# Earlier lanes, a two-pass ring for the last four groups, and scalings on VectorE in a fused attention and feed-forward kernel

## The chip, the cores and the metric

The kernel runs on one core of a Trainium2 chip. The metric is the device time of one execution in microseconds (us); the time before is the median of three runs. A profile is one further execution, recorded by the hardware profiler; times in it count from the start of its span. The engines are named as in the profile: PE is TensorE's matmuls, PEld its weight loads, DVE is VectorE, ACT is ScalarE, POOL is GpSimd, and SP is the engine that issues most DMAs.

## The reference

```python
x: (4, 12480, 128)  inducing: (32, 128)  w_in: (128, 2048)  w_out: (2048, 128)  alpha: (2048)
def mab(q, kv):
    a = softmax(q @ kv.T / sqrt(128))
    return a @ kv
h   = mab(inducing, x)         # per batch: 32 rows pool 12480 tokens
y   = mab(x, h)                # each token attends to the 32 rows
z   = y @ w_in
g   = max(z, 0) + alpha * min(z, 0)
out = g @ w_out                # (49920, 128), f32
```

## The kernel before

The kernel never forms `y`. It computes `hW = h @ w_in` once per batch (32 rows, repeated four times over the 128 partitions) and, for each token, the unnormalised weights `rep` of the 32 rows (also held four times). A product of a quarter of each, 32 rows deep, gives a chunk of 128 of the 2048 features for 512 tokens. The activation is split as `alpha*z + (1-alpha)*max(z,0)`, so the linear part needs one further product with `hA = h @ (w_in * alpha @ w_out)`, and only the relu part needs the 2048 features. The division by the softmax sum is left to the end, where it multiplies the output.

**Units.** Each batch has 25 groups: 24 of 512 tokens (numbers 0 to 23; four of them, one super tile, share their loads) and a remainder of 192 tokens (number 24). A group has 16 chunks. `fill` (L596) makes a chunk: one matmul on a quarter of the array (32 rows) into one of eight banks, and then a relu that brings it to bf16 in SBUF, on ScalarE (L614) or VectorE (L617). The planner keeps a clock for the three engines and gives the relu to the engine that it thinks is done first, from durations written by hand (`ca`, `cd` at L611). `piece` (L621) multiplies a chunk with the scaled output weights and adds to the group's own bank. A whole chunk can be summed in one full matmul of 128 rows (`whole`, L627), or in four quarter matmuls of 32 rows, one at a time.

**Lanes.** Quarter matmuls on the four row groups of the array run at the same time. Each row group is a lane. A laned group enters lane 0, has its 16 chunks' first quarters added there, then goes to lane 1 for the second quarters, and so on; up to four groups are in the lanes at once, one in each. Two lanes must not add to one bank at once, so before a group goes on, TensorE drains (L969, `hand_over`) and the first piece of the next lane waits for that drain's semaphore. Fills use slots of any lane. A chunk stays in SBUF until lane 3 has used it; at most `KEPT` are held. The loop from L976 chooses the next matmul by the planner's clock; `PLAN` has one letter per laned group, which sets four knobs of that choice (how hungry the eviction engines must be for a fill to go first, how many chunks may be left in lane 3 when a new group starts, what a fill costs an occupied lane, and whether a hand-over is made at once).

**Direct groups.** The first two groups, the four remainders, and groups 22 and 23 of batch 3 are direct, with whole sums. At the start there are eight *sessions* (L921): four fills at once, some tasks, then the four whole sums of the session before. A ninth set of four fills follows, and then the lanes begin. At the end, after the lanes have run empty, groups 22, 23 and 24 of batch 3 are summed whole (L1101); their fills are made before, in free lane slots.

**Tasks.** All other work (scores of the next super tile, its sums, loads and transposes for the next batch) stands in a table by time step, `at(t, ...)`. Steps up to 8 are the sessions; step T0 + m comes when the m-th laned group starts. If a step has matmuls, lanes pause there, because these matmuls use the whole array. At the start, `w_amat` (16 matmuls for `w_in * alpha @ w_out`), `h_linear` and the first two transposes of batch 1 stand in sessions.

**Finishing** (`finish`, L653): VectorE transposes the bank to SBUF (L664), GpSimd multiplies with the reciprocal sums (L667), and four DMAs write the result (L685). In the last batch DMAs of the last groups are issued by SP and ScalarE, and two of group 23 at the very end by GpSimd (L688). GpSimd also issues the loads of x.

Of the kernel before, what the change touches and what calls it, by code (L numbers as in the profile page):

```python
# [17 lines left out]
P = 128  # L18
NB = 4
GRP = P * NB  # L20
# [4 lines left out]
TAIL = 2  # L25
AHEAD = 8
LAND = 8000
KEPT = 62
RDS = 4
SLOT = 217  # L30
XTS = 9
DONE = 420
SWITCH = 110
# [4 lines left out]
PLAN = (  # L38
    "aaKKfGcyLqmADMamiiznjafamQcyaqcafqanqaxacmOaav"
    "AmnCamKeacfymraaJmRnAynqyauaNmmgadjmafycQazyAm"  # L40
)
# [3 lines left out]
def kernel(  # L45
# [550 lines left out]
    def fill(ch, f):  # L596
        b, g, u = ch
        st = states[b]
        pp, nb, cp = shape_of(g)
        t = pp * nb  # L600
        w = t * cp
        ps = bank()
        for i in range(cp):
            mm(
                ps[:, i * t : (i + 1) * t],
                st.hW[32 * f : 32 * f + 32, u * cp + i, :],
                st.rep[g][32 * f : 32 * f + 32, :t],
            )
        gt = gt_pool.tile([P, GRP], bf16, name="gt", tag="gt")
        after = 206 + w * 0.42  # L610
        ca, cd = 52 + w * 0.83, 74 + w * 1.04  # L611
        ready = clk.pe + after
        if max(clk.act, ready) + ca <= max(clk.dve, ready) + cd:
            pin(nc.scalar.activation(out=gt[:, :w], in_=ps[:, :w], func=RELU))  # L614
            drained(ps, "A", ca, after=after)
        else:
            pin(nc.vector.tensor_relu(gt[:, :w], ps[:, :w]))  # L617
            drained(ps, "D", cd, after=after)
        seen[ch] = gt, clk.free[number[id(ps)]]
# [28 lines left out]

    def flush():
        while held:  # L650
            finish(*held.pop(0))

    def finish(b, g):  # L653
        st = states[b]
# [9 lines left out]
        pin(nc.vector.transpose(out=ot[:, :t], in_=acc[:, :t]))  # L664
        drained(accs[b, g], "D", 74 + t * 1.04)
        ob = ob_pool.tile([P, GRP], f32, name="ob", tag="ob")
        pin(nc.gpsimd.tensor_tensor(  # L667
            out=ob[:, :t].rearrange("p (k m c) -> p k m c", k=nb, c=32),
# [153 lines left out]
    def tokens(st):  # L822
# [15 lines left out]
        tail = [y for y in direct[2:] if y[0] == B - 1]  # L838
# [21 lines left out]
        at(4, lambda: b_turn(st, 0))  # L860
        at(5, w_amat)
        at(6, lambda: h_linear(st))
        for b in range(B):
            base = T0 + (first[b, 0] if b else -2)
            for s in range(1, NS + 1):
                t = base + 4 * s - AHEAD - (b == 0 and s > 4) if b or s > 2 else 4 * s - 2
                nt = t + (5 if b == 0 and s == 2 else 3 if b == 0 and s == 4 else 4 if s < NS or b + 1 < B else 2)
                at(t, lambda b=b, s=s: b_scores(states[b], s))
                at(t + 1, lambda b=b, s=s: b_rep(states[b], s))
                at(nt, lambda b=b, s=s: b_den(states[b], s))  # L870
                at(nt + 1, lambda b=b, s=s: b_turn(states[b], s))
            if b + 1 < B:
                n = b + 1
                E = base + 4 * NS
                if b:
                    lag = (-8, -4, -4, 0, 4, 8, 8) if b > 1 else (-4, 0, 0, 4, 4, 8, 8)
                    score = [base + k for k in lag]
                    load = [t + k - 7 for t, k in zip(score, (0, 0, 2, 0, 1, 0, 2))]
                    cross = [t + k - 5 for t, k in zip(score, (0, 0, 1, 0, 1, 0, 2))]
                else:  # L880
                    score = [T0 + k for k in (2, 4, 4, 6, 9, 11, 13)]
                    load = [0, 0, 5, SESSIONS, T0 + 2, T0 + 4, T0 + 6]
                    cross = [None, None, 6, T0 + 1, T0 + 4, T0 + 7, T0 + 8]
# [4 lines left out]
                sums = [T0 + k for k in (4, 6, 6, 9, 11, 13, 14)] if n == 1 else [k + 4 for k in score]  # L888
                fs, fa = (t_scores, t_accum) if n == 1 else (a_scores, a_accum)
# [31 lines left out]
        for t in range(SESSIONS):  # L921
# [8 lines left out]
            prior = now  # L930
        for f in range(2):
            linear(0, f, f)
# [5 lines left out]
        finish(*held.pop(0))  # L938
        run_tasks(SESSIONS)
        flush()  # L940

# [12 lines left out]
        assert len(plans) == len(laned)  # L954
        fresh = {f: bank() for f in (2, 3)}

# [9 lines left out]
        def hand_over():  # L966
            nonlocal fenced
            if owed:
                pin(nc.tensor.drain(fusable=True)).then_inc(fence, 1)  # L969
                fenced += 1  # L970
            for y, f in owed:
                fences[y, f + 1] = fenced
                moving.append((y, f + 1, clk.pe + DONE))
            owed.clear()

        while queue or moving or owed or any(tile):  # L976
            best = []
            taken = {q for _, q, _ in moving} | {f + 1 for _, f in owed}
            for f in range(4):
                if tile[f]:  # L980
                    y, todo = tile[f]
                    if todo[0] is None:
                        best.append((free_at[f], 0, f, "linear"))
                    elif (*y, todo[0]) in seen:
                        t = max(free_at[f], seen[*y, todo[0]][1] - 100)
                        best.append((t, 1, f, "piece"))
                else:
# [4 lines left out]
                    if f == 0 and queue and lanes < LANES and (  # L992
                        lanes < LANES - 1 or room == KC or tile[3] and len(tile[3][1]) <= room
                    ):
                        ch = (*queue[0], 0)
                        if ch in seen:
                            t = max(free_at[f], seen[ch][1] - 100 - SLOT)
                            best.append((t, 2, f, "start"))
            if fillable():
                since = max(min(clk.free[i] for i in idle) - 40, landed.get(need[0][:2], 0))  # L1000
                hungry = min(clk.act, clk.dve) < clk.pe + hungry_at
                for f in range(4):
                    t = max(free_at[f], since)
                    if hungry:
                        best.append((t, 0.5 + 0.1 * bool(tile[f]), f, "fill", cost if tile[f] else 0))
                    elif not tile[f]:
                        best.append((t, 4 + (f in taken), f, "fill"))
            soon = min(max(x[0], clk.pe) for x in best) < clk.pe + 2 * SLOT
            for f in sorted(fresh):
# [7 lines left out]
            calm += [x for x in best if x[3] in ("warm", "spare")]  # L1017
            if owed and not best:
                hand_over()
                continue  # L1020
            if owed and not calm and at_once:
# [16 lines left out]
            if what == "start":  # L1038
# [34 lines left out]
            if what == "fill":  # L1073
                fill(need.pop(0), f)
            else:
                y, todo = tile[f]
                u = todo.pop(0)
                if u is None:
                    linear(*y, f)
                else:  # L1080
                    ch = (*y, u)
# [4 lines left out]
                    if f == 3:  # L1086
                        seen.pop(ch)
                    if not todo:
                        tile[f] = None
                        if f < 3:  # L1090
                            owed.append((y, f))
                        flush()
            free_at[f] = clk.pe + SLOT
# [51 lines left out]
```

## Time and profile before

| | us |
|---|---|
| median of 3 runs (559.07 to 559.81) | 559.15 |
| the profiled execution | 558.86 |
| its span | 557.1 |
| first fill | 25.38 |
| lanes begin | 41.7 |
| lanes end | 541.7 |
| last matmul ends | 550.6 |
| relus to SBUF: ScalarE 923, mean | 0.620 |
| relus to SBUF: VectorE 645, mean | 0.676 |
| transpose of a finished group, VectorE, mean of 96 | 0.710 |
| product with reciprocal sums, GpSimd, mean of 96 | 1.133 |

Means are durations of one instruction; those of an engine overlap, so that they follow each other a little faster. A matmul's duration includes its way through the array; the pace is seen in the starts. All of the helper `mm`'s matmuls have the line L138, so they are told apart by what they read: `rep,hW` is a fill, `gt,W` a piece or a whole sum, `W` alone an unneeded matmul in an empty lane.

### The profile page before, as it was taken

The numbers are of one execution on the slowest core, as the hardware profiler recorded it, in microseconds if no ns is written. First come the engines' busy times: TensorE is split into PE (matmuls) and PEld (weight loads), VectorE is DVE, ScalarE is ACT, GpSimd is POOL, SyncE is SP. The second block draws the span as 40 slices with busy tenths as digits, with TensorE's granted clock in tenths as the row PEclk, the third lists the DMA queues.
The fourth block names the chain that finished last, engine by engine and source line by source line (L and its number), as shares of the span: only waits on it lengthen the run. The fifth ranks groups of instructions, "written<-read, shape, count | busy, mean of one in ns | idle before, by whom it ended". The sixth has DMA issues, their size and how long they took to land.

```text
span 557.1 us, 21434 instructions
## 1 busy us (share of the span) xinstructions
PE 538.6 (97%) x8890; PEld 293.1 (53%) x8894; DVE 497.3 (89%) x858; ACT 503.8 (90%) x1008; POOL 411.4 (74%) x602
## 2 busy tenths in 40 slices
PE   4999999999999999999999999999999999999995
PEld 4645555555455555544555556554465554454642
DVE  3689999989999999999998999999998999999981
ACT  2479999999989999999999999999999999999980
POOL 6556466967898978878698878665668859767683
PEclk9999999999999999999999999999999999999999
DMA  9976999645999998687577996333334334333224
GB/s 196 230 136 142 134 192 176 132 94 89 151 199 165 176 144 164 148 120 150 102 131 131 169 170 140 64 93 88 75 81 112 73 81 118 65 94 65 47 62 75
DMA packets 110209, 69.25 MB, mean 124 GB/s; under 512 B 78800, under 2 KB 100672, under 8 KB 110112
## 3 DMA queue, kind: packets, MB, share of 16 engines
q0 software_dynamic: 23344, 38.66, 37.6%
q1 hardware_dynamic: 84624, 28.46, 26.3%
q8 instruction: 69, 1.13, 0.9%
q10 hardware_dynamic: 2144, 0.77, 0.5%
q14 instruction: 28, 0.23, 0.2%
HBM read 41.00 MB, written 28.95 MB: 126 GB/s over the span
## 4 chain that ended last, share of the span: by engine, by line
PE 31%; issue 27%; PEld 25%; POOL 8%; DMA 4%; ACT 3%; DVE 1%; PEldq 1%; POOLq 0%; DVEq 0%
PE bank L138 31%; PEld L138 25%; POOL out_dram L685 5%; DMA xn<-in_x_dram 3%; POOL ob L667 3%; ACT gt L614 2%; PEldq L969 1%; PE bank L226 1%; DMA out_dram<-ob 1%; DVE gt L617 1%; DVE hW L313 0%; POOL xn L180 0%; DVE ot L664 0%; DMA rt<-rd 0%; PEld bank L138 0%
## 5 line engine op out<-in xcount | busy, mean ns | idle before, releaser
L138 PE MATMUL bank<-gt,W 32*128 32x512 bf16 (+1 forms) x6013 | 482.9, 374 | 1.6 <-DVE gt L617 0.3
L614 ACT ACTIVATE gt<-bank 128x512 bf16<-128x512 f32 (+1 forms) x923 | 467.9, 620 | 14.3 <-PE bank L138 10.2
L617 DVE TENSOR_SCALAR gt<-bank 128x512 bf16<-128x512 f32 (+1 forms) x645 | 403.7, 676 | 19.9 <-PE bank L138 16.4
L138 PE MATMUL bank<-rep,hW 32*128 32x512 bf16 (+1 forms) x1600 | 417.9, 368 | 2.0 <-DVE hW L313 0.3
L138 PEld LDWEIGHTS <-W 32*128 32x128 bf16 (+1 forms) x6109 | 229.1, 92 | 188.0 <-issue 117.2
L685 POOL DMA_DIRECT2D out_dram<-ob x384 | 247.0, 673 | 36.9 <-POOL ob L667 27.8
L667 POOL TENSOR_TENSOR ob<-ot,rdT 128x512 f32<-128x512 f32 (+1 forms) x100 | 111.0, 1110 | 93.5 <-DVE ot L664 83.7
L138 PEld LDWEIGHTS <-hW 32*128 32x128 bf16 x1600 | 135.6, 91 | 31.3 <-issue 15.1
L664 DVE STREAM_TRANSPOSE ot<-bank 128x512 f32<-128x512 f32 (+1 forms) x100 | 69.7, 697 | 16.3 <-PE bank L138 15.0
L180 POOL DMA_DIRECT2D xn<-in_x_dram x70 | 40.4, 656 | 3.6 <-DMA xn<-in_x_dram 2.4
L138 PE MATMUL bank<-rep,hA 32*128 32x512 bf16 x94 | 35.0, 376 | 0.3 <-DVE hW L313 0.2
L232 DVE COPY xT<-bank 128x1024 bf16<-128x1024 bf16 (+1 forms) x16 | 10.8, 672 | 5.1 <-PE bank L226 4.9
L138 PE MATMUL bank<-W 32*128 32x512 bf16 x93 | 13.8, 376 | 0.0
L253 ACT ACTIVATE e1t<-bank 128x256 bf16<-128x256 f32 (+1 forms) x13 | 4.8, 372 | 9.7 <-PE bank L138 9.5
L138 PEld LDWEIGHTS <-hA 32*128 32x128 bf16 x94 | 8.5, 91 | 7.3 <-issue 4.8
L226 PE MATMUL bank<-ident,xn 128*128 128x128 bf16 x128 | 11.3, 242 | 0.9 <-DVE xn L786 0.9
L138 PE MATMUL bank<-xT,hT 128*32 128x512 bf16 (+1 forms) x98 | 10.4, 389 | 0.6 <-ACT gt L614 0.4
L498 ACT ACTIVATE e<-bank,rs 128x512 bf16<-128x512 f32 x12 | 8.4, 699 | 2.5 <-PE bank L138 2.3
L226 PEld LDWEIGHTS <-xn 128*128 128x128 bf16 x128 | 8.7, 109 | 2.2 <-DVE xn L786 1.0
L498 ACT ACTIVATE e<-bank 128x512 bf16<-128x512 f32 x12 | 7.4, 616 | 2.4 <-PE bank L138 2.4
L138 PE MATMUL bank<-IT,xT 128*128 128x32 bf16 x192 | 8.0, 179 | 0.2
L138 PEld LDWEIGHTS <-hT 128*32 128x32 bf16 (+1 forms) x122 | 5.0, 93 | 5.8 <-issue 4.0
(103 smaller groups left out, 144.4 us busy)
## 6 DMA issues: line engine op xcount, KB each, us to landing
out_dram<-ob POOLq DMA_DIRECT2D x374, 64.0 KB, 2.9
rep<-e2d SPq DMA_DIRECT2D x92, 128.0 KB, 3.3
xn<-in_x_dram POOLq DMA_DIRECT2D x48, 128.0 KB, 5.5
xn<-in_x_dram POOLq DMA_DIRECT2D x22, 256.0 KB, 6.9
e2d<-e SPq DMA_DIRECT2D x24, 128.0 KB, 3.1
rdT<-rt SPq DMA_DIRECT2D x96, 8.0 KB, 2.4
w_out_f<-in_moe_w_out_dram POOLq DMA_DIRECT2D x4, 256.0 KB, 11.2
xs<-in_x_dram SPq DMA_DIRECT2D x1, 512.0 KB, 4.8
```

The lines of the kernel that those rows point to most:

```text
L138: return pin(nc.tensor.matmul(o, lhsT, rhs, start=start, stop=stop, **kw))
L180: pin(nc.gpsimd.dma_start(out=xn[:, i * w : (i + 1) * w, :], in_=src[:, i * w : (i + 1) * w, :]))
L226: pin(nc.tensor.transpose(tp[:, k * P : (k + 1) * P], xn[:, q, j * C : (j + 1) * C], ident[:]))
L232: pin(nc.vector.tensor_copy(out=dst, in_=tp[:, :w]))
L253: pin(nc.scalar.activation(out=e1t[:pp, :nb, :].rearrange("p k m -> p (k m)"), in_=ps[:pp, : nb * M], func=EXP, scale=scale,))
L498: pin(nc.scalar.activation(out=e2[:].rearrange("p (t j i) -> p t j i", j=n, i=32), in_=turned(ps[:pp, :w], n), func=EXP, scale=scale_of(st ...
L614: pin(nc.scalar.activation(out=gt[:, :w], in_=ps[:, :w], func=RELU))
L617: pin(nc.vector.tensor_relu(gt[:, :w], ps[:, :w]))
L664: pin(nc.vector.transpose(out=ot[:, :t], in_=acc[:, :t]))
L667: pin(nc.gpsimd.tensor_tensor(out=ob[:, :t].rearrange("p (k m c) -> p k m c", k=nb, c=32), in0=ot[:, :t].rearrange("p (k m c) -> p k m c", ...
L685: pin(eng.dma_start(out=dst[a], in_=src))
L969: pin(nc.tensor.drain(fusable=True)).then_inc(fence, 1)
```

## The change

- Only group 0 is direct at the start; there are four sessions, and the lanes begin with group 1. `w_amat`, `h_linear`, the linear part of group 0 and all transposes of batch 1 go to the first starts of laned groups.
- The linear product of a laned group comes last, in lane 3, and no longer first, in lane 0.
- The last four laned groups (18 to 21 of batch 3, the *gang*) go through the lanes twice, with 8 chunks each time: from lane 3 back to lane 0. Their fills are ordered so: first halves of all four, then second halves.
- For the groups 23 and 24 of batch 3, VectorE makes the product with the reciprocal sums.
- The first two score sets get a tile of their own (`rep0`), and the buffer holds 60 chunks, not 62.
- The planner's durations are changed (`ca`, `cd`, `SLOT`, `DONE`, 7 ns per fill, 30 ns per linear), and the letters of `PLAN`. A start no longer counts the linear slot as cover for its first chunk.

```diff
+GANG = 4
+CUT = 8
-KEPT = 62
+KEPT = 60
-SLOT = 217
+SLOT = 218
-DONE = 420
+DONE = 450
 PLAN = (
...
-            st.rep0 = rep_pool.tile([P, NQ, GRP], bf16, name="rep", tag="rep")
+            st.rep0 = const.tile([P, 2, GRP], bf16, name="rep0")
...
-        ca, cd = 52 + w * 0.83, 74 + w * 1.04
+        ca, cd = 58 + w * 0.83, 77 + w * 1.04
...
-    def flush():
+    def flush(after=190):
...
-        drained(accs[b, g], "D", 74 + t * 1.04)
+        drained(accs[b, g], "D", 74 + t * 1.04, after=after)
         ob = ob_pool.tile([P, GRP], f32, name="ob", tag="ob")
-        pin(nc.gpsimd.tensor_tensor(
+        eng = nc.vector if b == B - 1 and g >= NG - 2 else nc.gpsimd
+        pin(eng.tensor_tensor(
...
-        direct = every[:2] + [(b, NG - 1) for b in range(B)] + every[-1 - TAIL : -1]
+        direct = every[:1] + [(b, NG - 1) for b in range(B)] + every[-1 - TAIL : -1]
...
-        need = [((first[y], 1, u), (*y, u)) for y in laned for u in range(KC)]
+        gang = laned[-GANG:]
+        need = [((first[y], 1, u), (*y, u)) for y in laned if y not in gang for u in range(KC)]
+        need += [
+            ((first[gang[i - i % LANES]], 1, u >= CUT, i, u), (*y, u)) for i, y in enumerate(gang) for u in range(KC)
+        ]
...
-        SESSIONS = 8
+        SESSIONS = 4
         T0 = SESSIONS + 1
...
-        at(5, w_amat)
-        at(6, lambda: h_linear(st))
+        at(T0, w_amat)
+        at(T0 + 1, lambda: h_linear(st))
+        at(T0 + 2, lambda: (linear_whole(0, 0), flush()))
         for b in range(B):
-            base = T0 + (first[b, 0] if b else -2)
+            base = T0 + (first[b, 0] if b else -1)
             for s in range(1, NS + 1):
-                t = base + 4 * s - AHEAD - (b == 0 and s > 4) if b or s > 2 else 4 * s - 2
+                t = base + 4 * s - AHEAD - (b == 0 and s > 4) if b or s > 2 else 2 * s
...
-                    at(7, lambda: p_xpose(states[1], 0, 0))
-                    at(SESSIONS, lambda: p_xpose(states[1], 0, 1))
-                    at(T0 + 2, lambda: p_xpose(states[1], 1, 0))
-                    at(T0 + 3, lambda: p_xpose(states[1], 1, 1))
+                    at(T0 + 1, lambda: p_xpose(states[1], 0, 0))
+                    at(T0 + 2, lambda: p_xpose(states[1], 0, 1))
+                    at(T0 + 3, lambda: p_xpose(states[1], 1, 0))
+                    at(T0 + 4, lambda: p_xpose(states[1], 1, 1))
...
-        fresh = {f: bank() for f in (2, 3)}
+        again = set()
+        fresh = {3: bank()}
...
-                fences[y, f + 1] = fenced
-                moving.append((y, f + 1, clk.pe + DONE))
+                fences[y, (f + 1) % 4] = fenced
+                moving.append((y, (f + 1) % 4, clk.pe + DONE))
...
-                            t = max(free_at[f], seen[ch][1] - 100 - SLOT)
+                            t = max(free_at[f], seen[ch][1] - 100)
...
-                tile[0] = [queue.pop(0), [None] + list(range(KC))]
+                y = queue.pop(0)
+                tile[0] = [y, list(range(CUT if y in gang else KC))]
                 continue
...
-                tile[f] = [x[0], list(range(KC))]
+                if x[0] in gang and x[0] not in again:
+                    tile[f] = [x[0], list(range(CUT))]
+                else:
+                    tile[f] = [x[0], list(range(CUT * (x[0] in again), KC)) + [None] * (f == 3)]
...
                 fill(need.pop(0), f)
+                clk.pe += 7
...
                     linear(*y, f)
+                    clk.pe += 30
...
-                    if not todo:
-                        tile[f] = None
-                        if f < 3:
-                            owed.append((y, f))
-                        flush()
+                if not todo:
+                    tile[f] = None
+                    if f == 3 and y in gang and y not in again:
+                        again.add(y)
+                        owed.append((y, f))
+                    elif f < 3:
+                        owed.append((y, f))
+                    flush(DONE)
```

More of the change, by code (lines that the diff above doesn't have):

```diff
@@ L38 @@
 PLAN = (
-    "aaKKfGcyLqmADMamiiznjafamQcyaqcafqanqaxacmOaav"
-    "AmnCamKeacfymraaJmRnAynqyauaNmmgadjmafycQazyAm"
+    "aKpuaKrsAmqacLyyjaclarAaAnCayemanGccjaosymyeyy"
+    "lAMjyaqyaKQemnimMjaanqqavyyrmamqymnqmameGcylay"
+    "j"
 )
@@ L647, in linear_whole, with finish @@
         spent(b, g, 1)
-    def flush():
+    def flush(after=190):
         while held:
-            finish(*held.pop(0))
-    def finish(b, g):
+            finish(*held.pop(0), after)
+    def finish(b, g, after):
         st = states[b]
@@ L837, in tokens @@
                 wholes[c + 1].append((b, NG - 1, u))
-        tail = [y for y in direct[2:] if y[0] == B - 1]
+        tail = [y for y in direct[1:] if y[0] == B - 1]
         tail.sort()
-        need = [((first[y], 1, u), (*y, u)) for y in laned for u in range(KC)]
+        gang = laned[-GANG:]
[3 more added lines that the diff above has]
+        ]
         need += [((c, 0, i), ch) for c, w in enumerate(wholes) for i, ch in enumerate(w)]
@@ L880, in tokens @@
                 else:
-                    score = [T0 + k for k in (2, 4, 4, 6, 9, 11, 13)]
-                    load = [0, 0, 5, SESSIONS, T0 + 2, T0 + 4, T0 + 6]
-                    cross = [None, None, 6, T0 + 1, T0 + 4, T0 + 7, T0 + 8]
-                    at(7, lambda: p_xpose(states[1], 0, 0))
-                    at(SESSIONS, lambda: p_xpose(states[1], 0, 1))
-                    at(T0 + 2, lambda: p_xpose(states[1], 1, 0))
-                    at(T0 + 3, lambda: p_xpose(states[1], 1, 1))
-                sums = [T0 + k for k in (4, 6, 6, 9, 11, 13, 14)] if n == 1 else [k + 4 for k in score]
+                    score = [T0 + k for k in (3, 5, 5, 7, 10, 12, 14)]
+                    load = [0, 0, SESSIONS, T0 + 1, T0 + 3, T0 + 5, T0 + 7]
+                    cross = [None, None, T0 + 1, T0 + 2, T0 + 5, T0 + 8, T0 + 9]
+                    at(T0 + 1, lambda: p_xpose(states[1], 0, 0))
+                    at(T0 + 2, lambda: p_xpose(states[1], 0, 1))
+                    at(T0 + 3, lambda: p_xpose(states[1], 1, 0))
+                    at(T0 + 4, lambda: p_xpose(states[1], 1, 1))
+                sums = [T0 + k for k in (5, 7, 7, 10, 12, 14, 15)] if n == 1 else [k + 4 for k in score]
                 fs, fa = (t_scores, t_accum) if n == 1 else (a_scores, a_accum)
@@ L930, in tokens @@
             prior = now
-        for f in range(2):
-            linear(0, f, f)
         for f in range(4):
@@ L937, in tokens @@
             whole(ch)
-        finish(*held.pop(0))
         run_tasks(SESSIONS)
-        flush()
         clk.pe += SWITCH
@@ L977, in tokens @@
             best = []
-            taken = {q for _, q, _ in moving} | {f + 1 for _, f in owed}
+            taken = {q for _, q, _ in moving} | {(f + 1) % 4 for _, f in owed}
             for f in range(4):
@@ L982, in tokens @@
                     if todo[0] is None:
-                        best.append((free_at[f], 0, f, "linear"))
+                        if hasattr(states[y[0]], "hA"):
+                            best.append((free_at[f], 0, f, "linear"))
                     elif (*y, todo[0]) in seen:
@@ L1007, in tokens @@
                         best.append((t, 4 + (f in taken), f, "fill"))
+            if owed and not best:
+                hand_over()
+                continue
             soon = min(max(x[0], clk.pe) for x in best) < clk.pe + 2 * SLOT
@@ L1017, in tokens @@
             calm += [x for x in best if x[3] in ("warm", "spare")]
-            if owed and not best:
-                hand_over()
-                continue
             if owed and not calm and at_once:
@@ L1087, in tokens @@
                         seen.pop(ch)
-                    if not todo:
-                        tile[f] = None
-                        if f < 3:
-                            owed.append((y, f))
-                        flush()
+                if not todo:
[6 more added lines that the diff above has]
+                    flush(DONE)
             free_at[f] = clk.pe + SLOT
```

## The prediction

> **What bounds the kernel now.** I read four views in this order: the page's busy times, the chain that ended last, the busy time by stretch, and the order of time on VectorE, TensorE and GpSimd in the last 30 us.
>
> The page first:
>
> ```profile
> span 557.1 us, 21434 instructions
> PE 538.6 (97%) x8890; PEld 293.1 (53%) x8894; DVE 497.3 (89%) x858; ACT 503.8 (90%) x1008; POOL 411.4 (74%) x602
> ...
> PE 31%; issue 27%; PEld 25%; POOL 8%; DMA 4%; ACT 3%; DVE 1%; PEldq 1%; POOLq 0%; DVEq 0%
> ...
> L614 ACT ACTIVATE gt<-bank 128x512 bf16<-128x512 f32 (+1 forms) x923 | 467.9, 620 | 14.3 <-PE bank L138 10.2
> L617 DVE TENSOR_SCALAR gt<-bank 128x512 bf16<-128x512 f32 (+1 forms) x645 | 403.7, 676 | 19.9 <-PE bank L138 16.4
> ```
>
> The chain names TensorE and its issue for most of the span, but matmuls overlap, so a busy PE is not a full one. Where only unneeded matmuls ran beside one lane (540.3 to 541.4), sets of four started every 0.2175 us: 0.054 us for a quarter-array matmul. The 60.0 to 509.1 stretch holds 7582 matmuls, 59 ns each. The other two engines drain what fill makes: 923 + 645 evictions.
>
> ```profile
> core 0: us, PE busy (x) PEld busy (x) DVE busy (x) ACT busy (x) POOL busy (x), PEclk, DMA share, GB/s
> 25.40:34.00 8.60, 7.84 (x56) 2.65 (x57) 7.43 (x14) 7.50 (x15) 8.60 (x11) 1.00 0.46 116
> 34.00:41.70 7.70, 7.21 (x73) 3.60 (x72) 6.46 (x14) 4.86 (x9) 1.32 (x3) 1.00 1.02 175
> 41.70:51.90 10.20, 10.20 (x157) 4.58 (x156) 9.64 (x16) 9.52 (x19) 6.25 (x9) 1.00 0.59 132
> 60.00:509.10 449.10, 445.98 (x7582) 239.51 (x7575) 421.40 (x722) 434.88 (x875) 345.00 (x487) 1.00 0.66 124
> ```
>
> These are the second half of the sessions, the first lanes and the steady state. ScalarE is busy 97% and VectorE 94% of the steady state: **the evictions bound it**, with TensorE close behind. From 34.0 to 41.7 VectorE was idle 1.24 us and ScalarE 2.84 us: the sessions feed evictions worse than lanes do.
>
> The end is another regime. On VectorE, and then on GpSimd:
>
> ```profile
> 534.78 0.71 DVE L664 STREAM_TRANSPOSE ot<-bank 128x512 f32<-128x512 f32 x1
> ...
> 538.38 0.69 DVE L664 STREAM_TRANSPOSE ot<-bank 128x512 f32<-128x512 f32 x1
> 539.00 1.45 DVE L617 TENSOR_SCALAR gt<-bank 128x384 bf16<-128x384 f32 x3
> 541.86 0.72 DVE L664 STREAM_TRANSPOSE ot<-bank 128x512 f32<-128x512 f32 x1 [1.42 <-PE bank L138]
> ...
> 549.33 0.72 DVE L664 STREAM_TRANSPOSE ot<-bank 128x512 f32<-128x512 f32 x1 [2.95 <-PE bank L138]
> 550.70 0.38 DVE L664 STREAM_TRANSPOSE ot<-bank 128x192 f32<-128x192 f32 x1 [0.66 <-PE bank L138]
> ```
> ```profile
> 550.13 1.55 POOL L667 TENSOR_TENSOR ob<-ot,rdT 128x512 f32<-128x512 f32 x2 [2.59 <-DVE ot L664]
> 551.62 1.29 POOL L688 DMA_DIRECT2D out_dram<-ob  x2
> ```
>
> The last eviction ends at 540.45 on VectorE and 541.16 on ScalarE, but TensorE works until 550.6: it finishes the last laned group at 541.7 and then sums groups 22, 23 and 24 of batch 3 whole for 8.9 us. Both eviction engines have nothing left then.
>
> **The change, part by part.** Sums are against the profiled execution's 558.86 us (span 557.1, 1.76 outside it); the median of the runs shown, 559.15, is 0.29 above, which I add at the end.
>
> *Start.* The first fill is at 25.38; sessions 0 to 4 start at 25.4, 27.0, 29.0, 30.8 and 32.1. After the change the fifth set of fills and the last whole sums (to 33.4), one score set (0.33, from the row at 36.66) and the switch lead into the lanes at about 33.9, not 41.7: 7.7 us earlier, with one group fewer done. By TensorE the extra laned group costs a steady lane stage, (509.1 - 61.3)/87 transposes of finished groups = 5.15 us, and the work taken out of the sessions goes into pauses of the lanes: the 16 matmuls for Amat 0.9, four halves of transposes of which two are new there 1.1, h_linear and the whole linear 0.4, and three switches at 0.3: 2.9 us. That way it is -7.7 + 5.15 + 2.9 = +0.3. By the evictions, which bind, the four sessions removed hold an idle of (1.24 + 2.84)/2 = 2.0 us; three new pauses leave about 0.4 each (at the first lane pause, 51.6 to 53.4, VectorE lost 0.62 and ScalarE 0.19): -2.0 + 1.2 = -0.8. Ends: +0.3 (or +1.0 if each pause costs 0.6), and -2.4 if the pauses hide. I take **-0.7**, nearest to the eviction count. `linear` moved to lane 3 is one matmul per group either way: 0. It needs hA some 10 us after h_linear has made it. The rep0 tile of its own frees a buffer for the second load of rep; the trace shows no wait for one, so 0. SP and GpSimd get the same DMAs in the same order; only score set 2 and the loads of batch 1 are earlier by two or so sessions, on queues idle from 35 to 45 us (GpSimd).
>
> *Tail.* Groups 18 to 21 of batch 3 are the gang. They finish at 531.05, 534.78, 538.38 and 541.86: the last three stages have nothing behind them and take 3.73, 3.60 and 3.48 us, against 16 slots of 0.2175 = 3.48. So the drain is at the lanes' own pace, at 3, 2 and 1 lanes filled, and evictions for the tail fill beside it. With two passes of 8 chunks the drain's stages have 8 slots. That doesn't shorten the sum of stages by itself: the ring has 8 stages of 8 slots = 13.9 us after the group ahead of it has left (524.17 now), instead of 4 + 3 stages of 16. What it buys is that in the three stages before it only 8 chunks per group must be ready, not 16, so those three can run faster than now (509.1 to 524.2, 15 us, of which 10.4 are slots). I take half of the way from 521 (4 us a stage) to 524.2: 522.5. Eight stages at 1.74 plus 0.25 for handing over (the surplus of the first drain stage, 3.73 - 3.48) make 15.9: the lanes end at 538.4, which the evictions allow: the gang's last chunk is ready by about 529 (42 evictions follow, and 40 are the tail's), plus 0.6 and three drain stages is 535.6. At 538.4 some 7 tail chunks are unfilled ((540.4 - 538.4) x 3.4 per us); two fill sets between whole sums cost 2 x (0.22 + 0.2) = 0.8. TensorE ends at 538.4 + 0.3 + 8.9 + 0.8 = 548.4 instead of 550.6: **-2.2**. Ends: -4.1 (lanes end at 535.6, four fill sets) and +3.8 (rival B).
>
> *Scalings.* No f32 product of this size runs on VectorE now. Rows of tensor-by-scalar from PSUM give 342 ns for 128 columns and 744 for 512, so 1.05 ns a column; from the 287 ns of a 128-column sum, 512 columns come to 0.69 us, 192 to 0.35. Bounds: 0.29 (a sum of 128 columns) and 1.13 (GpSimd's). Group 23 is then ready at 550.05 + 0.69 = 550.74 instead of 551.16, the remainder at 551.1 + 0.35 = 551.45 instead of 551.67, and the two late DMAs no longer wait for GpSimd's products. The issues on ScalarE's queue (0.74 each, last at 552.8) follow the first: **-0.4**, between +0.1 and -0.7. The Trainium skill ("VectorE: DVE Perf Modes", the walkthrough of the modes) says an f32 product of two tensors has no faster mode than one element per cycle of 0.96 GHz; I estimate 0.53 us plus start from that page, which would make this -0.5.
>
> *Durations and table.* They change only which engine takes which chunk and in which order. Evictions really follow each other at 0.50 (ScalarE, 19 in 9.61 us) and 0.61 (VectorE, 12 in 7.42); the old formula says 0.477 and 0.606, the new one 0.483 and 0.610. That is nearer, by little. The steady idle is 27.7 and 14.2 us, mean 21; a table that moves a tenth of it gives -2.1 or +2.1. I take 0. Two kept chunks fewer cost nothing while evictions bind, since the buffer is then not full; their cover is that lanes wait for chunks, and without it the fills stop sooner in each pause.
>
> Sum: -0.7 - 2.2 - 0.4 = -3.3, so 555.6, and by the median 555.9 us.
>
> **Rivals.** *A, the ring eats its own gain.* For: every entry into a lane needs a fence, and TensorE's drain at line 969 lasts 0.42 to 0.87 us, median 0.55; eight-slot stages give it half the cover, and in a ring all four lanes stand at a boundary together. At 5 us of exposed fences the lanes end at 541.4 as now, and no fills are left: tail 0, sum -1.1: 558.1. Against: the drain stages now show 0.12 to 0.25. The Trainium skill ("TensorEngine Tiling (Array Packing)", Key Properties) says that changing the tiling mode drains the array. This speaks against whole sums broken by fills and against the new pauses; the trace agrees, with 0.30 us from the last lane matmul (541.38) to the first whole one (541.68) where the pitch is 0.22, and I already count 0.1 for each change.
>
> *B, slower.* The same place, but the 16 added entries (four groups, four lanes) each stand alone with the drain's median: 16 x 0.55 = 8.8 us in TensorE's queue, where fills wait too. TensorE ends at 522.5 + 13.9 + 8.8 + 0.3 + 8.9 = 554.4, so +3.8; with the other parts +2.7: 561.9. It makes the kernel slower by 0.2% from 0.45 us per added entry on. For: the queue is in order, so that a fence stops fills as well. Against: only 19 drains are in the whole trace, so most entries share one or hide it.
>
> *C, all covers hold.* Pauses hide (-2.4), the lanes end with the evictions (-4.1), scalings -0.5: 552.1. For: evictions lead at both ends. Against: TensorE's count at the start.
>
> **Numbers.** About 0.2% (1.1 us) is what a measurement of this kernel can tell from no change. Forecast 0.57 (own range 553.0 to 558.5, with the table's 2.1 either way), C 0.15, A 0.12, B 0.16. Faster takes the first two and 0.05 of A: 0.77; same 0.07; slower B: 0.16. The range must reach C and A and leave most of B out: 551.2 to 560.2.
>
> **What would show it.** Start: the first quarter-array piece at 33.9 (now 42.1), group 1 transposed by about 56. Tail: the last lane piece near 538.4, whole sums broken by fills, TensorE's end near 548.4 while the last evictions still end near 540. Scalings: two products of about 0.7 and 0.35 us on VectorE, the last DMA issue 0.4 us nearer to TensorE's end. Steady state: 5.15 us per finished group. I am wrong if that pace moves by over 0.03 us, if the lanes don't end ahead of the last evictions, or if evictions at the start idle as much as in the sessions.

## The result, and the profile after

The changed kernel takes 561.13 us (median of 20 executions, 558.93 to 566.94); the kernel before 559.21 (median of 20, 558.79 to 561.41). The ratio is 1.0042, with a 95% interval of 1.0023 to 1.0060: slower by 0.4%, where 0.6% faster was forecast. The range given, 551.2 to 560.2, doesn't hold it. Not only the median moved: single times now spread over 8.0 us, before over 2.6.

The profiled execution after took 564.29 us, which is above the median, so that it shows the loss enlarged. Its page, with the chain that ended last:

```profile
span 562.5 us, 21453 instructions
PE 536.6 (95%) x8886; PEld 288.5 (51%) x8890; DVE 494.9 (88%) x853; ACT 506.3 (90%) x1015; POOL 409.7 (73%) x600
...
PE 51%; issue 16%; PEld 11%; POOL 9%; DMA 7%; ACT 4%; PEldq 1%; SPq 1%; DVE 1%; ACTq 0%; POOLq 0%; DVEq 0%
```

Every engine is busy for the same time as before, to within 2.5 us; the 5.4 us that the span grew are idle time. POOL and DMA have grown in the chain. The stretches say where, set against those of before (start and end of the lanes):

```profile
34.00:41.70 7.70, 7.70 (x108) 4.58 (x109) 7.19 (x16) 7.35 (x15) 2.38 (x5) 1.00 1.04 186
...
543.60:552.50 8.90, 8.85 (x51) 4.68 (x51) 1.88 (x4) 1.08 (x3) 7.64 (x12) 1.00 0.30 61
552.50:562.50 10.00, 0.04 (x1) 0.00 (x0) 2.06 (x4) 0.00 (x0) 2.42 (x4) 0.71 0.52 89
```

From 34.0 to 41.7 VectorE and ScalarE are now idle 0.5 and 0.35 us (columns after PE and PEld), not 1.24 and 2.84: the start does what it should. But the last stretch, after TensorE's last matmul, is 10.0 us long and was 6.5.

Transposes of finished groups, counted in order, place the loss. Compared with before, group 2 of batch 0 is done 1.9 us earlier (59.46, not 61.34), and the 17th transpose 2.2 us earlier (136.83, not 139.05). Later the changed kernel falls behind: the 32nd comes 5.4 us later than before (219.55, not 214.17), the 56th 5.8 (344.97, not 339.20). Single differences swing by some us, since the two kernels finish groups in different orders (the 33rd is only 2.0 us later). The clean mark is run e7 below, a version with the same order and no such wait: against it the changed kernel loses nothing up to the 30th transpose, then 4.3 us at the 31st and 1.6 more at the 56th. At these two places TensorE stands still. Who waited for whom, on TensorE's matmuls (columns: total us, times, the longest):

```profile
PE bank L141 <- DMA xT<-xn: 4.1, 2, 2.6
```

and at its own DMA queue, SP. First the kernel before, then the changed one:

```profile
SPq L516 <- PE bank L138: 6.3, 18, 0.5
```
```profile
SPq L519 <- PE bank L141: 120.0, 21, 10.6
```

L516 and L519 are the same statement, the load of `rep`. In the kernel before it hardly ever waits for TensorE; now it waits 120 us in total. Part of this only replaces a wait that SP had anyway: its waits for the reciprocal sums, which VectorE makes, went down at the same time. Before, and then changed:

```profile
SPq L549 <- DVE rd L544: 142.0, 17, 16.9
```
```profile
SPq L552 <- DVE rd L547: 86.0, 20, 10.3
```

So it is not the total that costs, but where the load comes too late for what stands behind it. `rep` has three buffers, a super tile of four groups in each. A buffer is free when the last matmul that reads it is done. Before, the linear product came while fills of its group were still to come, so that the last fill freed the buffer; now it is the linear product, which stands behind the last piece in lane 3, some three stages later. SP works in order, and behind that load stands the transpose of x for the next batch. SP's queue around the first stall, in the changed kernel:

```profile
190.04 1.82 SPq L562 DMA_DIRECT2D rdT<-rt  x4
198.49 1.74 SPq L519 DMA_DIRECT2D rep<-e2d  x4
200.41 3.02 SPq L197 DMA_TRANSPOSE xT<-xn  x1
```

and in an execution of the version with a fourth buffer, where TensorE doesn't wait (run e7 below):

```profile
191.08 1.84 SPq L562 DMA_DIRECT2D rdT<-rt  x4
192.97 3.82 SPq L519 DMA_DIRECT2D rep<-e2d  x4
197.75 3.78 SPq L197 DMA_TRANSPOSE xT<-xn  x1
```

The load goes out 5.5 us later and the transpose 2.7. It lands 8.0 us after its issue, at 208.4; the scores that read it stand at the head of TensorE's queue from 205.9 and start at 208.45. The need has moved as well: in the kernel before, the transpose went out at 198.50, landed 7.8 us later, and was read from 208.49 on. The changed kernel is ahead there and wants it 2.6 us earlier, so the spare time of 2.2 us was gone before the load came late. At the second stall the transpose is issued at 332.29, not 324.77.

The end, on VectorE and then on GpSimd, in the changed kernel:

```profile
538.17 0.71 DVE L667 STREAM_TRANSPOSE ot<-bank 128x512 f32<-128x512 f32 x1
...
540.07 0.71 DVE L667 STREAM_TRANSPOSE ot<-bank 128x512 f32<-128x512 f32 x1
...
542.47 0.70 DVE L667 STREAM_TRANSPOSE ot<-bank 128x512 f32<-128x512 f32 x1
...
544.04 0.72 DVE L667 STREAM_TRANSPOSE ot<-bank 128x512 f32<-128x512 f32 x1
548.01 0.72 DVE L667 STREAM_TRANSPOSE ot<-bank 128x512 f32<-128x512 f32 x1 [3.25 <-POOL ob L671]
552.64 0.72 DVE L667 STREAM_TRANSPOSE ot<-bank 128x512 f32<-128x512 f32 x1 [3.92 <-POOL ob L671]
...
554.24 0.38 DVE L667 STREAM_TRANSPOSE ot<-bank 128x192 f32<-128x192 f32 x1
558.05 0.36 DVE L671 TENSOR_TENSOR ob<-ot,rdT 128x192 f32<-128x192 f32 x1 [3.43 <-DMA out_dram<-ob]
```
```profile
538.96 1.08 POOL L671 TENSOR_TENSOR ob<-ot,rdT 128x512 f32<-128x512 f32 x1 [7.82 <-DVE ot L667]
540.34 2.57 POOL L689 DMA_DIRECT2D out_dram<-ob  x4 [0.30 <-POOL ob L671]
542.83 1.17 POOL L671 TENSOR_TENSOR ob<-ot,rdT 128x512 f32<-128x512 f32 x1
544.30 2.57 POOL L689 DMA_DIRECT2D out_dram<-ob  x4 [0.30 <-POOL ob L671]
546.80 1.18 POOL L671 TENSOR_TENSOR ob<-ot,rdT 128x512 f32<-128x512 f32 x1
548.94 2.58 POOL L689 DMA_DIRECT2D out_dram<-ob  x4 [0.96 <-POOL ob L671]
551.43 2.20 POOL L671 TENSOR_TENSOR ob<-ot,rdT 128x512 f32<-128x512 f32 x2
```

The gang's four groups finish within 5.9 us (538.17 to 544.04); before, they came every 3.5 to 3.7 us. GpSimd needs about 4 us for each of the first three: a product and four DMA issues of 0.65. Its products of groups 21 and 22 begin at 551.43, although group 21's transpose ended at 544.8. VectorE's two `ot` buffers are full meanwhile, so that group 23's transpose waits 3.92 us. The last product (192 columns) then waits 3.43 us for an output buffer whose DMA went out late.

### The profile page after: what moved, and what is told of

Same layout as the page of the kernel before. It is cut to its first block, busy times and chain, and to the rows that moved or that the text cites. A ratio compares the mean times of both kernels' runs of the same rounds, so it can differ in the third digit from the quotient of the medians.

```text
span 562.5 us, 21453 instructions
## 1 busy us (share of the span) xinstructions
PE 536.6 (95%) x8886; PEld 288.5 (51%) x8890; DVE 494.9 (88%) x853; ACT 506.3 (90%) x1015; POOL 409.7 (73%) x600
## 3 DMA queue, kind: packets, MB, share of 16 engines
q8 instruction: 69, 1.13, 0.9%
## 4 chain that ended last, share of the span: by engine, by line
PE 51%; issue 16%; PEld 11%; POOL 9%; DMA 7%; ACT 4%; PEldq 1%; SPq 1%; DVE 1%; ACTq 0%; POOLq 0%; DVEq 0%
PE bank L141 51%; PEld L141 11%; POOL out_dram L689 5%; ACT gt L617 4%; DMA xn<-in_x_dram 3%; POOL ob L671 3%; DMA out_dram<-ob 1%; DMA rep<-e2d 1%; DMA xT<-xn 1%; PEldq L975 1%; POOL xn L183 1%; SPq L519 1%; PE bank L229 1%; DVE hW L316 0%; PEld bank L141 0%
## 5 line engine op out<-in xcount | busy, mean ns | idle before, releaser
L141 PE MATMUL bank<-gt,W 32*128 32x512 bf16 (+2 forms) x6062 | 480.5, 375 | 1.5 <-DVE hW L316 0.3
L617 ACT ACTIVATE gt<-bank 128x512 bf16<-128x512 f32 x930 | 471.2, 617 | 11.2 <-PE bank L141 8.2
L141 PE MATMUL bank<-rep,hW 32*128 32x512 bf16 (+1 forms) x1600 | 424.8, 368 | 1.8 <-issue 0.3
L620 DVE TENSOR_SCALAR gt<-bank 128x512 bf16<-128x512 f32 x638 | 400.8, 677 | 23.4 <-PE bank L141 18.9
L141 PEld LDWEIGHTS <-W 32*128 32x128 bf16 (+1 forms) x6105 | 222.9, 92 | 188.3 <-issue 118.9
L671 POOL TENSOR_TENSOR ob<-ot,rdT 128x512 f32<-128x512 f32 (+1 forms) x98 | 109.3, 1117 | 92.8 <-DVE ot L667 81.6
L141 PEld LDWEIGHTS <-hW 32*128 32x128 bf16 x1600 | 137.2, 91 | 34.7 <-issue 16.1
L330 ACT ACTIVATE e<-bank 128x512 bf16<-128x512 f32 x12 | 7.4, 622 | 3.6 <-issue 3.6
L141 PE MATMUL bank<-W 32*128 32x512 bf16 x41 | 10.3, 376 | 0.0
L501 ACT ACTIVATE e<-bank 128x512 bf16<-128x512 f32 x12 | 7.5, 622 | 2.7 <-PE bank L141 2.7
L141 PE MATMUL bank<-xT,IT 128*32 128x512 bf16 x48 | 4.7, 393 | 4.1 <-DMA xT<-xn 4.1
```

The lines of the kernel that those rows point to most:

```text
L141: return pin(nc.tensor.matmul(o, lhsT, rhs, start=start, stop=stop, **kw))
L330: pin(nc.scalar.activation(out=e1[:], in_=ps[:], func=EXP, scale=scale, accum_out=st.es[:, u : u + 1]))
L501: pin(nc.scalar.activation(out=e2[:].rearrange("p (t j i) -> p t j i", j=n, i=32), in_=turned(ps[:pp, :w], n), func=EXP, scale=scale_of(st ...
L671: pin(eng.tensor_tensor(out=ob[:, :t].rearrange("p (k m c) -> p k m c", k=nb, c=32), in0=ot[:, :t].rearrange("p (k m c) -> p k m c", k=nb, ...
```

## The experiments

Theory R: the linear product at the end holds `rep` longer, and late transposes stall TensorE. Theory Q: GpSimd's queue at the end. Rival G: the ring's fences, or the new order as such, lose the time. Times are medians; ratios are to the kernel before, run on the same chip, with 95% intervals. It took 559.45 us beside e1 to e3 and "before, linear last", 559.82 beside e4 to e7 and 559.10 beside e8 to e11, so a difference of medians across these sets carries up to 0.7 us of its own.

| run | edit | us | ratio |
|---|---|---|---|
| e1 | changed, linear product first | 574.47 | 1.0272 [1.0254, 1.0290] |
| e2 | changed, tail's DMAs on SP | 558.69 | 0.9986 [0.9959, 1.0014] |
| e3 | e1 and e2 | 571.62 | 1.0212 [1.0199, 1.0225] |
| before, linear last | one part alone | 582.75 | 1.0408 [1.0392, 1.0424] |
| e4 | changed, 4 rep buffers | 558.66 | 0.9998 [0.9973, 1.0023] |
| e5 | e4 and e2 | 554.55 | 0.9910 [0.9891, 0.9929] |
| e6 | e5, one pass | 558.09 | 0.9978 [0.9961, 0.9996] |
| e7 | e5, scalings on GpSimd | 554.91 | 0.9910 [0.9894, 0.9925] |
| e8 | e4, 4 output buffers | 558.74 | 0.9996 [0.9980, 1.0012] |
| e9 | before, new letters | 578.25 | 1.0337 [1.0324, 1.0351] |
| e10 | e5, one letter | 597.59 | 1.0688 [1.0673, 1.0704] |
| e11 | e10, linear first | 591.69 | 1.0590 [1.0573, 1.0607] |

**e1, the linear product first again.**

```diff
-                tile[0] = [y, list(range(CUT if y in gang else KC))]
+                tile[0] = [y, [None] * (m > 0) + list(range(CUT if y in gang else KC))]
...
-                    tile[f] = [x[0], list(range(CUT * (x[0] in again), KC)) + [None] * (f == 3)]
+                    tile[f] = [x[0], list(range(CUT * (x[0] in again), KC)) + [None] * (f == 3 and x[0] == laned[0])]
```

> The changed kernel with the linear product back at the front, in lane 0, for every laned group but the first one (which still has it last, since hA is not there yet). Theory R (a super tile's rep buffer is read by the linear products, so with them last in lane 3 the buffer is held some three stages longer, SP waits with the next load of rep, and the transposes queued behind it come late): SP's wait for TensorE at the loads of rep falls from 120 us to under 20 us, TensorE's wait for transposed x (4.1 us in the changed kernel's profile) to under 0.5 us, and the time from 561.1 to about 558 us with a spread below 1.5 us. Rival G (the fences of the two-pass ring, or the table of orders, make the loss): the waits may change, the time stays within 0.7 us of 561.1.

SP's wait for TensorE at this load fell to 5.1 us, TensorE's wait for transposed x was gone, and the times lay within 2.4 us (1.5 was expected). So far R holds. But the time was 574.5, not 558. Moving one matmul shifts the planner's clock, and every later choice of order comes out differently; the letters were made for another sequence. This run can't say what the place of the linear product is worth. e9 to e11 take up that doubt.

**e2, the tail's DMAs on SP.**

```diff
-        ending = b == B - 1 and g >= NG - 4
+        ending = b == B - 1 and g >= NG - 8
```

> The changed kernel with the output DMAs of groups 17 to 20 of the last batch issued by SP and not by GpSimd (as it already is for 21 and 22). Theory Q (the ring finishes its four groups 1.6 to 2.4 us apart, but GpSimd needs 1.1 us for the product and 2.6 us for four DMA issues, some 4 us a group; its backlog delays the last transposes and the last product): the stretch from TensorE's last matmul to the end of the span falls from 10.0 us to about 7, VectorE's waits for GpSimd (7.2 us) and for the free buffer (3.4 us) nearly vanish, and the time falls by about 3 us to 558. Rival G: the end of TensorE's work, not the finish, is late; less than 1 us is won.

2.4 us faster than the changed kernel by the medians. The stretch after TensorE's end was 5.6 us in its profile, and both waits had gone. Q holds. Times still spread from 556.0 to 564.5. The profiled execution is the longest of them (564.47; without it the median is 558.24), and in it TensorE waits 6.1 us for transposed x: R's loss is untouched.

**e3, both.**

> The changed kernel with both edits: linear product first in lane 0, and the DMA issues of groups 17 to 20 of the last batch on SP. R and Q together: about 555.5 us, and the lanes end near 538.5 as was predicted. If only one of them is right, about 558; if G is right, 560 to 561.

2.9 us faster than e1: Q again, under another order. The sum of 555.5 was missed, as was e1's 558, by its spoiled order.

**The kernel before, with the linear product last.** The edit is `list(range(KC)) + [None] * (f == 3)` in place of `[None] + list(range(KC))`, and the two statements that it needs.

> The kernel before with the linear product last, in lane 3, and nothing else of the change (the order table is the old one; it was not made for this). Theory R: SP's wait for TensorE at the loads of rep grows from 6.3 us to 60 us or more, transposed x comes late in some runs, and the time grows by 1 to 3 us with a wider spread. Rival G: within 0.7 us of the kernel before.

SP's wait grew from 6.3 to 114.7 us, as R says, and 1.8 us of waiting for transposed x appeared. The time grew by 23 us, far more than R accounts for. A spoiled order, as in e1, is the likely rest; this run doesn't separate the two.

**e4, a fourth rep buffer.** Nothing else changes, above all not the order of any engine.

```diff
-    rep_pool = ctx.enter_context(tc.tile_pool(name="repp", bufs=3))
+    rep_pool = ctx.enter_context(tc.tile_pool(name="repp", bufs=4))
```

> The changed kernel with four buffers for rep instead of three, and no other line changed, so every engine's order of instructions is the same. Theory R (the linear product at the end holds the rep buffer longer, SP waits, transposed x is late in some runs): SP's wait for TensorE at the loads of rep falls from 120 us to under 15 us, TensorE no longer waits for transposed x, the spread falls from 8 us to under 1.5 us, and the median to about the fastest runs of the changed kernel, 558.9 us. Rival S (the waits only take up slack; the loss in the middle is the new order's): the waits fall but the median stays above 560.5.

SP's wait fell to 5.4 us, and the median by 2.5 us to 558.66, the fastest executions of the changed kernel. Its interval touches that of the changed kernel (1.0023), so this pair alone doesn't settle it; e2 against e5, the same edit with the tail cured, does: 558.69 to 554.55, with intervals far apart. The spread was not cured as expected: three of twelve executions were above 562.8, and the profile still has one wait of 1.2 us for transposed x at 206 us:

```profile
193.71 5.29 SPq L519 DMA_DIRECT2D rep<-e2d  x4
199.27 3.53 SPq L197 DMA_TRANSPOSE xT<-xn  x1
```
```profile
206.90 0.40 PE L141 MATMUL bank<-xT,IT 128*32 128x512 bf16 x4 [1.25 <-DMA xT<-xn]
```

The load of `rep` is early here, as in e7, but the transpose goes out only 1.1 us earlier than in the changed kernel. The chain that leads to this stall goes through an output DMA on GpSimd's queue (193.71 to 199.27), for which the transpose waited, and not through `rep`. e5 and e6 have such a wait too (1.8 and 1.2 us), and e8 two; e7 has none. So the fourth buffer cures the wait for `rep` and shortens the stalls, but it doesn't bring back the spare time. Why the transpose goes out at 197.75 in one execution and at 199.2 to 200.4 in others was not tried.

**e5, both cures.**

> The changed kernel with four rep buffers and the output DMAs of groups 17 to 20 of the last batch on SP. R and Q (GpSimd's queue at the end, worth 2.9 us between the first and the third run above): 556 us, the best so far, with a spread below 1.5 us. If Q overlaps with R: 557.5 or more.

554.55 us, 0.9% faster than the kernel before and the best version here; R and Q don't overlap. The times lie within 2.2 us, not 1.5. Its end, on VectorE:

```profile
543.59 0.72 DVE L667 STREAM_TRANSPOSE ot<-bank 128x512 f32<-128x512 f32 x1 [2.92 <-PE bank L141]
547.23 0.72 DVE L667 STREAM_TRANSPOSE ot<-bank 128x512 f32<-128x512 f32 x1 [2.92 <-PE bank L141]
548.04 0.69 DVE L671 TENSOR_TENSOR ob<-ot,rdT 128x512 f32<-128x512 f32 x1
548.65 0.38 DVE L667 STREAM_TRANSPOSE ot<-bank 128x192 f32<-128x192 f32 x1
549.06 0.36 DVE L671 TENSOR_TENSOR ob<-ot,rdT 128x192 f32<-128x192 f32 x1
```

The releaser is TensorE again, and each product follows its transpose. TensorE ends at 548.5 and the span at 554.1: 5.6 us, where it was 6.5 before and 10.0 in the changed kernel.

**e6, one pass.** The edit on e5 is `gang = []` in place of `gang = laned[-GANG:]`.

> The run with four rep buffers and the tail on SP, and no gang: the last four laned groups pass the lanes once, with 16 chunks. The order is the same up to those groups. The step of the prediction (two passes end TensorE's work 2.2 us earlier): 2 to 2.5 us slower than the two-pass version, with the drain's stages back at 3.5 us. Rival (two passes only move idle slots): within 0.6 us of it.

3.5 us slower than e5. But the letters of the last groups were made for two passes, and the last drain stage of this run took 6.4 us (transposes at 537.10 and 543.46), not 3.5: the last group worked alone in the lanes for some 25 slots, not 16. With 3.5 us in its place the run would be only 0.6 us slower than e5, which is the rival's bound. So two passes are worth between 0.6 and 3.5 us; how much was not shown.

**e7, scalings back on GpSimd.** The edit on e5 is `eng = nc.gpsimd`.

> The run with four rep buffers and the tail on SP, and the last two scalings back on GpSimd. The prediction's step says 0.4 us slower than with them on VectorE. Rival (GpSimd is no longer in the way once SP issues): within 0.15 us.

0.36 us slower by the medians, as the step said, but the intervals overlap: likely, not shown. No matmul waited for transposed x in its profiled execution, so it served above as the undisturbed trace.

**e8, a fourth output buffer**, on e4: `name="obp", bufs=4`, and `bufs=KEPT - 1` for the chunks.

> The changed kernel with four rep buffers, four instead of three buffers for scaled output tiles (ob), and 59 instead of 60 chunk buffers in SBUF to make room (the planner's order is unchanged). DMA issues of the tail stay on GpSimd. It splits the loss at the end: if the last product's wait of 3.4 us for a free ob buffer is what costs, 555.5 us, nearly as good as with the issues on SP; if GpSimd's queue itself sets the end (its wait only takes another form), 558 or more, as with four rep buffers alone.

No gain (558.74). VectorE's wait for an output buffer went away, its 7.2 us of waits for GpSimd stayed, and nine output DMAs of the last groups now left SP's queue in a row from 550.4 to 557.1. The queue sets the end, not the buffer. Its profile also has waits of TensorE for transposed x at both of the old places (1.1 and 1.4 us), with four `rep` buffers.

**e9 to e11, what the letters are worth.** e9 is the kernel before with the last 92 of the new letters; e10 is e5 with `PLAN = "a" * 93`; e11 is e10 with the edit of e1.

> The kernel before with the letters of the new order table (its last 92), all else unchanged but for one statement of the planner moved up as in the change so that it can go through. The first run above with the linear product first was 13.4 us slower than the changed kernel although its waits had gone. Theory T (a table fits only the schedule that it was made for): 5 to 25 us slower than the kernel before. Rival (the letters matter little, and the place of the linear product is what cost 13 us): within 2 us of the kernel before.

> The run with four rep buffers and the tail on SP, with the same letter for every laned group. Theory T: 8 to 20 us slower than with its table (554.6). Rival: within 3 us.

> As the run with one letter for every group, but with the linear product first, in lane 0, for all laned groups but the first. With no tuned table on either side this compares the two places. Theory T (the place itself costs nothing once there are buffers): within 2 us of the run with the linear product last. Rival (the place costs): 8 us or more slower.

The new letters make the kernel before 19 us slower; with one letter for all groups e5 loses 43 us, over twice what was expected. So a table is worth tens of us, a table made for another schedule can cost as much, and e1's 13 us need no other cause, though that this is theirs was not shown. With one letter the linear product in lane 0 is 5.9 us faster than in lane 3, against both theories (within 2 us, or 8 or more slower). Whether that is the place or the chance of two untuned orders stays open.

## Why the prediction was wrong

**The start came out as forecast, as far as it can be told.** -0.7 was forecast, between -2.4 and +1.0. Group 1 is transposed at 54.85 (about 56 was said), and in the undisturbed trace of e7 the third to the 17th transpose come 0.2 to 2.2 us earlier than before. (TensorE's count in the working, by its own terms, adds up to 3.3 us of moved work and not 2.9, so to +0.75; the forecast went by the evictions and doesn't hang on it.)

**The step that failed first:** "`linear` moved to lane 3 is one matmul per group either way: 0", with "SP and GpSimd get the same DMAs in the same order". Both sentences can be true, and they ask the wrong thing. What counts is when the matmul lets go of what it reads. It came before the last fills of its group and became the last reader of `rep`, three stages later; that turned 6.3 us of SP's waits for TensorE into 120, and transposes behind them came late, at a place where being ahead had already used up the spare time. Cost by the medians: 2.5 us (changed kernel against e4), or 4.1 with the tail cured (e2 against e5; 3.7 without e2's longest execution). The same sentence on rep, "the trace shows no wait for one, so 0", looked at the buffers for the change that frees one and not for the change that holds them.

**The step that failed second** is the tail's, by what it left out. TensorE's own part came out near the forecast: from the transpose at 509.1 to TensorE's end the kernel before takes 550.6 - 509.1 = 41.5 us, and the changed one, from the transpose of the same number, 552.5 - 513.3 = 39.2 us: -2.3, forecast -2.2. Some of this is luck. The mark is coarse, because the orders differ: counted from the transpose after it, the difference is -2.9. And two parts of the sum are off in opposite directions: from that mark to the last matmul in the lanes it takes 30.0 us in the changed kernel and in e5, where 29.3 was forecast, and what follows takes 9.2, not 10.0, because no fill comes between the whole sums. But what stands after TensorE's end was taken as fixed but for -0.4. The working had the numbers: groups finishing 3.5 us apart, and on the page 1.13 us for a product and 0.67 for each of four issues, some 4 us a group. Groups that finish faster than that fill GpSimd's queue; the ring made them come 1.6 to 2.4 us apart, and the working itself had 1.99 for a stage. Cost: 2.4 us (e2), 2.9 (e1 to e3) or 4.1 (e4 to e5). What is late next was asked of TensorE alone.

**Scalings:** the products take 0.69 and 0.36 us, forecast 0.69 and 0.35. In the changed kernel the gain is buried under the wait of 3.43 us; with the queue cured, 0.36.

**Durations and table:** 0 came out right for the order itself: from the third to the 90th transpose a group takes 5.147 us before and 5.150 in e7. (In the changed kernel, with its two stalls, it is 5.217, beyond the 0.03 us that the prediction allowed.) But 2.1 us either way was far too sure of the letters. They are worth 43 us against one letter for all, and a wrong set costs 19. That the new set kept the pace was shown by the run, not by anything in the profile before.

**Rivals.** B gave 561.9 and the measured time is near it, by chance: its fences don't show. The trace has 18 drains, where it had 19, and their median is 0.54 us. A rests on the same fences. With both failed steps cured the time is 554.55, against 559.82 for the kernel before beside it: -5.3 us, where -3.3 was forecast for a kernel without these waits. Which of the start, the steady state and the ring made the other 2 us was not separated.

## What to carry to other kernels

When an instruction moves later, list what it reads and ask when those buffers come free, and then what stands behind the load that waits for one in its queue, however little the instruction itself costs. A kernel that gets ahead also wants its loads earlier, so ask what spare time each load has left. When the producers of a stage are made to finish closer together, compare their new spacing with what the stage behind them needs for each, from product to DMA issue. A tuned order table is a part of the schedule: an experiment that changes the order must keep the table's fit or measure its loss, and edits that leave the order alone (a buffer more, another queue) are the clean ones.

## What the hardware showed

A stall of TensorE can cost more than its length. Around the first stall of the changed kernel, by stretch (PEclk is the granted clock):

```profile
core 0: us, PE busy (x), PEclk, DMA share, GB/s
206.00:208.00 2.00, 0.00 (x0) 1.00 0.53 107
208.00:210.00 2.00, 1.55 (x16) 0.65 0.88 160
210.00:212.00 2.00, 2.00 (x24) 0.50 0.33 66
212.00:214.00 2.00, 2.00 (x39) 1.00 0.18 17
```

TensorE idled for 2.6 us, and then ran at half its clock until about 212: matmuls of 0.37 us took 0.63. Against e7, the changed kernel lost 4.3 us between the 30th and the 31st transpose: 2.6 of waiting and the rest in the slow stretch. In e2's profile 4.65 us of waiting were followed by some 6 us at 0.50. Waits of 1.2 us (e4) and 1.5 (the second stall) left the clock at 1.00. In between, the length does not decide. The kernel before with the linear product last, and then e5:

```profile
347.71 0.62 PE L138 MATMUL bank<-xT,IT 128*32 128x512 bf16 x4 [1.78 <-DMA xT<-xn]
```
```profile
348.00:350.00 2.00, 2.00 (x24) 0.50 0.80 151
```
```profile
207.63 0.40 PE L141 MATMUL bank<-xT,IT 128*32 128x512 bf16 x4 [1.79 <-DMA xT<-xn]
```
```profile
208.00:210.00 2.00, 2.00 (x44) 1.00 0.92 141
```

After 1.78 us of waiting the clock was at 0.50 until about 351; after 1.79 us it stayed at 1.00. This would fit the spread of single executions (the two longest of the changed kernel, 565.9 and 566.9 us, have its two lowest mean clocks, 0.990 and 0.987; between the others the order is not so clear): a DMA that comes a little later may tip the clock. The Trainium skill ("TensorE: Matmul & The Clock Gate", Part 1) says that the clock halves after at least one idle window of some 3.4 us, in windows that run freely. The traces agree on the half (0.50) and on the chance in it (1.78 against 1.79 us); the drop came here after 2.6 and 1.8 us of idleness already.
